# Q loaded on 64 partitions by nine tokens per pair of heads, in an attention and feed-forward kernel

## The chip, the cores and the metric

The kernel runs on one core of a Trainium2 chip. The metric is the device time of one execution in microseconds. TensorE (PE) does the matmuls; VectorE (DVE), ScalarE (ACT) and GpSimd (POOL) work on elements; SyncE (SP) here only issues transfers. Transfers go through 16 DMA engines, in queues that SP, ACT and POOL feed.

## What is computed

```
q, k, v: (8, 8, 576, 64)           # batch, head, token, head_dim; f32
q_s = softmax of q over the 64 elements of a token's head
k_s = softmax of k over the 576 tokens, per element
kv  = einsum('bhsd,bhse->bhde', k_s, v)
x   = einsum('bhsd,bhde->bhse', q_s, kv)   # then (batch * token, head * 64) = (4608, 512)
h   = x @ w_in                     # (512, 2048)
g   = where(h > 0, h, exp(min(h, 0)) - 1)
out = g @ w_out                    # (2048, 512)
```

## The kernel before

One batch is 576 tokens. Its first 512 (`SM`) make one **block** of the feed-forward, and the 64 tokens left over of each of the eight batches (`SR`) are gathered in `XTR` and make a ninth block. A block has 16 steps. In step s, `hidden` makes 128 of the 2048 hidden units for 512 tokens (four matmuls of 128x512 with `W1S`, line 778), ACT takes the exp, POOL a minus one, `elu` on DVE writes `GT`, and `project`, some three steps later, adds that chunk to the four output banks (four matmuls with `W2S`, line 799). After the sixteenth projection `store` copies the four banks to `OSB` and SP writes each of them out, 128 rows of 512 floats.

The attention of batch j+1 is made while block j runs, by **words** in tables: `FIRST` for block 0, `SECOND` for block 1, `LATER` for the others with `CHANGED` over it in block 2. Each step has three strings of words: done after `hidden`, after `project`, and after `elu`. `START` is the list for batch 0, which runs ahead of everything. Every engine works in the order in which the words are met, and `op` puts the waits in by itself, from what was last written and read. So the order of the words is the order of every queue, SP's among them: a transfer on SP's queue that has to wait for a buffer holds those behind it.

The words that matter here:

- `load:Q:2:MR` loads q of batch j+2 (lines 265 to 284). Part A is heads 0 to 3, B is 4 to 7, M both. A partition holds four tokens in a row of each head: 1024 bytes in a piece, 128 partitions. Part R is the 64 tokens left over, in two loads of 64 partitions with 256 bytes a piece. K and V are loaded in the same way. `QR` and `KR` have two buffers, `VR` one.
- `qmax`, `qsub`, `qexp`, `qsum`, `qmul` are the softmax of q, in parts of heads; `qmul` writes `QS` in float16, `qmulr` the rest piece `QSR`.
- `turn:A`, `turn:B`, `turn:R` transpose `QS` to `QW` by DMA on SP's queue, eight, eight and two blocks of 128x128; `wide` copies them to `QT` in float32. `pturn` and `pwide` do the same by TensorE and a bank, for batches 0 and 1.
- `peak`, `join`, `kout`, `kin` find the maximum of k per element and spread it over the partitions through a scratch in DRAM (`kmax_scratch`). For batches 0 and 1 it is done by `kmax`, `kturn`, `kacross`, `diag` and, for batch 1, `kspread`, on DVE and TensorE.
- `ksub`, `kexp`, `vconv`, `kv`, `kfac` make the 64x64 matrices of the heads, in `MB`.
- `att:f` and `xc:f` apply `MB` to a pair of heads' 512 tokens and copy the result to `XT`; `rest0` and `rcopy0` do the rest tokens. `flat:0` to `flat:4` with `xflat` go over the four pairs' 2304 columns in five cuts, rest tokens among them, and `xrest` takes these out to `XTR`. Batches 0 and 1 have the first form, the others the flat one.
- `w1:a:b` and `w2:a:b` load weights on POOL's queue; `warm` runs matmuls on constants; `hold` makes SP wait for the last `hidden`.

Of the kernel before, what the change touches and what calls it, by code (L numbers as in the profile page):

```python
# [27 lines left out]
AB = 7  # L28
# [6 lines left out]
AT = {"rawA": 0, "rawA2": 1, "rawB": 5, "rawB2": 2, "rawS": 6, "rawT": 3,  # L35
      "kturnA": 6, "kturnB": 7, "kvA": 3, "kvB": 6, "pturnA": 7, "pturnB": 3,
      "att0": 5, "att1": 7, "att2": 6, "att3": 4}
START = ("load:K:0:A kmax:A warm:2:6 kraw:A load:Q:0:A load:K:0:R load:K:0:B qmax:A qsub:A:gp kmax:S "
         "kturn:A kacross:A load:V:0:R warm:4:5 qexp:A kmax:B kraw:S load:Q:0:B kmax:T qmax:2 "
         "kturn:B diag:act:A kacross:B load:V:0:B diag:act:B w1:2:4 qmax:3 kraw:T kmin:S w1:0:2 "  # L40
         "kmin:T kmin:A w1:4:6 qsub:2:gp qexp:2 qsum:A kraw:B kexp:T vconv:B:gp kexp:S qsub:3:gp "
         "kmin:B qmul:A:dve kexp:A qexp:3 await:gp:DGA qsum:2 vconv:R:gp load:V:0:A qsum:3 w2:0:1 "
         "kexp:B vconv:A:gp w2:1:2 w1:6:8 pturn:A w2:2:3 kv:A pwide:A:act kfac:A:dve qmul:3:dve "
         "warm:1:5 kv:B att:0 qmul:2:dve att:1 xc:0 load:K:1:R pturn:B kfac:B:dve w2:3:5 load:K:1:M "
         "xc:1 pwide:B:act h:2:4 await:sp:VBA w1:8:10 w2:5:9 att:3 att:2 load:Q:1:A h:0:2 w1:10:14 "
         "xc:2 kmax2:B xc:3 load:Q:0:R kmax2:A kmax2:R ")
FIRST = {
    0: ("", "", ""),
    1: ("qmax:A", "", "load:Q:1:B"),
    2: ("", "", ""),  # L50
    3: ("qsub:0", "qsub:1:dve", ""),
    4: ("", "qexp:A", "qmax0:R qsub0:R:dve"),
    5: ("kturn qsum:A load:Q:1:R kacross w2:9:12", "qexp0:R", "qmul:A"),
    6: ("diag w1:14:16 qmax:C", "qsub:2:dve hold", "qsub:D:dve"),
    7: ("", "", "load:V:1:RAB"),
    8: ("kspread copy", "qexp:C qsum0:R", "ksub:3 qmulr0:dve"),
    9: ("ksub:0 pturn:A", "ksub:2:dve qsum:C", "pwide:A:act"),
    10: ("", "pturn0:R ksub:1:dve ksub:R pwide0:R:act", "vconv:R"),
    11: ("qmul:B:dve rest0", "w2:12:13 vconv:A:dve rcopy0:act", "kexp:A"),
    12: ("pturn:B load:K:2:MR qmulr:gp", "", "kexp:R pwide:B:act hold"),  # L60
    13: ("kv:A load:Q:2:ABR w2:13:16 kfac:A:dve kexp:B", "vconv:B:gp att:0", "xc:0 turn:R peak2:A"),
    14: ("kv:B peak2:R kfac:B:dve", "peak2:B att:1 join2", "xc:1"),
    15: ("att:3 xc:3", "att:2 load:V:2:MR", "kout2 xc:2"),
}
SECOND = {
    0: ("qmax:A", "qsub:1:dve qsub:0", ""),
    1: ("wide0:R:dve qmax:C", "qsub:D", "qexp:A"),
    2: ("rest0", "kin", ""),
    3: ("", "", "qsub:2"),
    4: ("qexp:C", "qsum:A qmul:0", ""),  # L70
    5: ("", "qsum:C", "ksub:R:dve ksub:3"),
    6: ("ksub:2:dve", "load:K:2:MR vconv:B", ""),
    7: ("", "qmulr:dve", "load:Q:2:MR qmul:1"),
    8: ("", "qmul:B:dve", "peak2:A vconv:R"),
    9: ("", "turn:R ksub:A kexp:B", "vconv:A"),
    10: ("kexp:R", "kexp:A", "turn:B"),
    11: ("", "peak2:B", "turn:A wide:R:gp rcopy0:act"),
    12: ("", "wide:B:act wide:A:gp kv:AB", "kfac:AB:dve"),
    13: ("", "flat:0 peak2:R", "xflat:0:act"),
    14: ("flat:1 xflat:1:dve load:K:3:MR", "join2 flat:2", "xflat:2:act"),  # L80
    15: ("flat:3", "xflat:3:dve flat:4", "qmax2:A xflat:4:act load:V:2:MR kout2 xrest:gp"),
}
LATER = {
    0: ("qsub:2", "", ""),
    1: ("qsub:1:dve", "kin", ""),
    2: ("qsub:0", "", ""),
    3: ("", "qexp:A ksub:R:dve ksub:0:dve", "qsum:A"),
    4: ("", "qsub:D", "kexp:R qmul:A:dve"),
    5: ("", "turn:A", "vconv:B"),
    6: ("ksub:3 qexp:C", "ksub:1 vconv:R", "vconv:A"),  # L90
    7: ("ksub:2:dve", "qsum:C", "qmulr:dve qmul:B:dve"),
    8: ("load:V:2:MR kexp:A", "kexp:B", ""),
    9: ("turn:R", "", "wide:A:gp turn:B"),
    10: ("kv:AB kfac:AB:dve", "peak2:A", ""),
    11: ("flat:0 xflat:0:act", "load:Q:3:MR", "peak2:B wide:R:act"),
    12: ("wide:B:dve", "flat:1 peak2:R xflat:1:act", ""),
    13: ("join2 load:K:3:MR", "", "flat:2 qmax2:C xflat:2:act"),
    14: ("", "flat:3 kout2", "xflat:3:act qmax2:A"),
    15: ("flat:4", "xflat:4:act", "xrest:dve"),
}  # L100
CHANGED = {
    0: ("", "", "qmax:C qsub:0"),
    2: ("", "", "qsub:2 load:Q:2:MR"),
# [13 lines left out]
class Gen:  # L117
# [57 lines left out]
    def alloc(self):  # L175
# [89 lines left out]
    def load(self, which, b, parts, en="sp"):  # L265
# [3 lines left out]
        t, e = bufs[s], self.E[en]  # L269
        for part in parts:  # L270
# [299 lines left out]
    def qgroups(self, part):  # L570
        return {"A": slice(0, 16), "B": slice(16, 32), "R": slice(32, 36), "C": slice(16, 36),
                "D": slice(24, 36)}.get(part) or slice(8 * int(part), 8 * int(part) + 8)

    def qstat(self, name, part):
        cells = {"A": "01", "B": "23", "C": "23R", "D": "3R"}.get(part, part)
        return [f"{name}{x}" for x in cells]

    def qkeys(self, b, part):
        s = b % 2
        r = [f"QR{s}R0", f"QR{s}R1"]  # L580
        cells = {"A": "01", "B": "23", "C": "23", "D": "3", "R": ""}.get(part, part)
        return [f"QR{s}{x}" for x in cells] + (r if part in "RCD" else [])

    def qmax(self, b, part):
        v, QR, g = self.E["dve"], self.QR[b % 2], self.qgroups(part)
        self.op("dve", lambda: v.tensor_reduce(self.QM[:, g], QR[:, g, :], AX.X, ALU.max),  # L586
                self.qkeys(b, part), self.qstat("QM", part))

    def qsub(self, b, part, en="gp"):
        e, QR, g = self.E[en], self.QR[b % 2], self.qgroups(part)  # L590
        n = g.stop - g.start
        m = self.QM[:, g].unsqueeze(2).broadcast_to([128, n, 64])
        keys = self.qkeys(b, part)
        self.op(en, lambda: e.tensor_tensor(QR[:, g, :], QR[:, g, :], m, ALU.subtract),  # L594
                keys + self.qstat("QM", part), keys)

    def qexp(self, b, part):
        a, QR, g = self.E["act"], self.QR[b % 2], self.qgroups(part)
        keys = self.qkeys(b, part)
        self.op("act", lambda: a.activation(QR[:, g, :], QR[:, g, :], AF.Exp), keys, keys)  # L600

    def qsum(self, b, part):
        v, QR, g = self.E["dve"], self.QR[b % 2], self.qgroups(part)
        self.op("dve", lambda: v.tensor_reduce(self.QZ[:, g], QR[:, g, :], AX.X, ALU.add),  # L604
                self.qkeys(b, part), self.qstat("QZ", part))
        self.op("dve", lambda: v.reciprocal(self.QI[:, g], self.QZ[:, g]),
                self.qstat("QZ", part), self.qstat("QI", part))

    def qmul(self, b, part, en="gp"):
        e, QR = self.E[en], self.QR[b % 2]  # L610
        g = self.qgroups(part)
        h0, n = g.start // 4, (g.stop - g.start) // 4
        src = QR[:, g, :].rearrange("p (h r) d -> p h r d", r=R)
        z = self.QI[:, g].rearrange("p (h r) -> p h r", r=R).unsqueeze(3).broadcast_to([128, n, R, 64])
        out = self.QS[h0 // 4][:, :, h0 % 4:h0 % 4 + n, :].rearrange("p r h d -> p h r d")
        keys = self.qkeys(b, part)
        cells = {"A": "01", "B": "23"}.get(part, part)
        self.op(en, lambda: e.tensor_tensor(out, src, z, ALU.mult),  # L618
                keys + self.qstat("QI", part), [f"QS{x}" for x in cells])

    def qmul_rest(self, b, en="gp"):
        e, QR = self.E[en], self.QR[b % 2]
        z = self.QI[:, 32:36].unsqueeze(2).broadcast_to([128, 4, 64])
        self.op(en, lambda: e.tensor_tensor(self.QSR[:, :, :], QR[:, 32:36, :], z, ALU.mult),
                self.qkeys(b, "R") + ["QIR"], ["QSR"])

    def qturn(self, part):

        sp = self.E["sp"]
        if part in "AB":  # L630
            hh = 0 if part == "A" else 1
            src = self.QS[hh][:, :, :, :].rearrange("p r h d -> p (r h d)")
# [24 lines left out]
    def qwide_first(self, part, bank, en="act"):  # L657
# [377 lines left out]
```

## Time and profile before

| what | value |
|---|---|
| time, median of 3 runs | 314.96 us (314.33 to 315.04) |
| the profiled execution: time, span | 315.17 us, 313.4 us |
| mean granted TensorE clock | 0.995 |
| first `hidden` matmul of block 0 | 20.1 us |
| first issue of the stores of blocks 0 to 6 | 66.3, 98.5, 129.9, 161.2, 192.5, 223.8, 255.1 us |
| first `hidden` matmul of the ninth block | 278.3 us |
| DMA: moved, mean rate | 51.63 MB, 165 GB/s |
| q loads, by DMA issue: 1024 KB, 512 KB, 64 KB | 5 of 6.7 us, 6 of 5.6 us, 16 of 6.5 us to landing |
| output stores: 256 KB | 2.8 us to landing |

The span is from the first to the last instruction of the profiled execution; the time has a little more around it. The stores of a block are issued in step 3 of the next one, so their distance is the length of a block: 31.3 us from the third on. "To landing" is from the issue of a transfer to its last byte, a median over those of one shape.

### The profile page before, as it was taken

The page shows a single profiled execution, that of the slowest core. Times are in us where ns is not written, and L with a number is a line of the kernel's source. Part 1 is how long each engine was busy: PE and PEld are TensorE (multiplying, and loading weights), DVE is VectorE, ACT ScalarE, POOL GpSimd, SP SyncE. Part 2 cuts the span into 40 slices and gives each one's busy share as a digit, 9 for nine tenths or more (in the row PEclk, how much of TensorE's full clock was granted, in tenths as well). Part 3 has the DMA queues.
Part 4 walks back from the last instruction along what each step waited for, and adds up shares of the span by engine and source line. Part 5 has one row for each costly group of instructions (what it writes and reads, how often), then busy time and mean ns, then how long its engine had stood idle before and what let it go on. Part 6 is the DMA issues. An engine that isn't in the chain of part 4 may idle for free.

```text
span 313.4 us, 4541 instructions
## 1 busy us (share of the span) xinstructions
PE 300.6 (96%) x1604; PEld 238.2 (76%) x1604; DVE 246.6 (79%) x422; ACT 178.8 (57%) x298; POOL 165.8 (53%) x224
## 2 busy tenths in 40 slices
PE   5988789999999999999999999999999999999995
PEld 2557567688878878887888788878888888888884
DVE  6897798989898999899989998999898353435531
ACT  1675558465846855685568556855685543334432
POOL 2975847277725843684368436843684233333330
PEclk9999979999999999999999999999999999999999
DMA  8999996959784897429842974270422030003003
GB/s 234 325 353 337 367 349 189 285 172 284 156 238 149 207 279 216 147 61 238 253 152 56 270 221 153 51 191 1 157 47 42 0 127 9 0 2 135 0 1 134
DMA packets 65079, 51.63 MB, mean 165 GB/s; under 512 B 29344, under 2 KB 57248, under 8 KB 65056
## 3 DMA queue, kind: packets, MB, share of 16 engines
q1 hardware_dynamic: 57984, 41.23, 47.1%
q0 software_dynamic: 5872, 8.39, 9.9%
q10 hardware_dynamic: 1200, 1.72, 1.6%
q8 instruction: 12, 0.20, 0.3%
q14 instruction: 11, 0.09, 0.1%
HBM read 38.27 MB, written 9.45 MB: 152 GB/s over the span
## 4 chain that ended last, share of the span: by engine, by line
PE 85%; DMA 6%; POOL 4%; SPq 2%; DVE 1%; issue 1%; ACT 1%; DVEq 0%
PE bank L799 41%; PE bank L778 39%; DMA QR<-in_q_dram 6%; PE bank L709 2%; PE bank L535 1%; POOL QR L594 1%; SPq L276 1%; POOL VB L515 1%; DVE QM L586 1%; POOL W1S L253 1%; SPq L284 0%; POOL W2S L260 0%; PE bank L687 0%; PE bank L652 0%; PE bank L539 0%
## 5 line engine op out<-in xcount | busy, mean ns | idle before, releaser
L767 POOL TENSOR_SCALAR ES<-ES 128x512 f32<-128x512 f32 x144 | 92.0, 641 | 130.0 <-ACT ES L766 129.8
L799 PE MATMUL bank<-W2S,GT 128*128 128x512 f32 x576 | 156.2, 395 | 1.1 <-DVE GT L789 0.8
L778 PE MATMUL bank<-XT,W1S 128*128 128x512 f32 x512 | 139.6, 394 | 2.7 <-DVE GT L789 2.4
L766 ACT ACTIVATE ES<-bank 128x512 f32<-128x512 f32 x144 | 85.1, 597 | 95.6 <-PE bank L778 95.3
L789 DVE SCALAR_TENSOR_TENSOR GT<-bank,ES 128x512 fp32r<-128x512 f32 x144 | 97.7, 680 | 50.1 <-PE bank L778 39.0
L799 PEld LDWEIGHTS bank<-W2S,GT 128*128 128x128 f32 x576 | 107.2, 189 | 23.6 <-DVE GT L789 1.2
L778 PEld LDWEIGHTS bank<-XT,W1S 128*128 128x128 f32 x512 | 95.0, 189 | 23.4 <-DVE GT L789 2.9
L594 POOL TENSOR_TENSOR QR<-QR,QM 128x512 f32<-128x512 f32 (+2 forms) x22 | 26.5, 1205 | 6.2 <-DVE QM L586 6.2
L600 ACT ACTIVATE QR<-QR 128x1024 f32<-128x1024 f32 (+3 forms) x18 | 19.0, 1057 | 12.1 <-POOL QR L594 7.7
L586 DVE TENSOR_REDUCE QM<-QR 128x16 f32<-128x1024 f32 (+3 forms) x18 | 21.7, 1205 | 2.1 <-DMA QR<-in_q_dram 2.1
L604 DVE TENSOR_REDUCE QZ<-QR 128x16 f32<-128x1024 f32 (+3 forms) x18 | 21.7, 1204 | 0.0
L731 ACT ACTIVATE XT<-bank 128x512 fp32r<-128x512 f32 (+2 forms) x28 | 15.4, 551 | 10.9 <-PE bank L709 10.9
L414 POOL TENSOR_TENSOR KR<-KR,NB 128x512 f32<-128x512 f32 (+1 forms) x14 | 21.3, 1539 | 0.0
L618 DVE TENSOR_TENSOR QS<-QR,QI 128x1024 f16<-128x1024 f32 (+1 forms) x15 | 18.5, 1241 | 0.0
L778 PE MATMUL bank<-XTR,W1S 128*128 128x512 f32 x64 | 16.6, 389 | 0.0
L367 DVE TRANSPOSE_TENSOR_REDUCE KM<-KR 128x32 f32<-128x1024 f32 x12 | 14.8, 1234 | 0.0
L452 ACT ACTIVATE EK<-KR 128x1024 bf16<-128x1024 f32 x14 | 14.2, 1056 | 0.4 <-POOL KR L414 0.4
L778 PEld LDWEIGHTS bank<-XTR,W1S 128*128 128x128 f32 x64 | 12.0, 188 | 2.5
L517 ACT ACTIVATE VB<-VR 128x1024 bf16<-128x1024 f32 x12 | 12.7, 1056 | 0.1
L709 PEld LDWEIGHTS bank<-QT,MB 128*128 128x128 f32 x48 | 8.9, 188 | 4.0 <-DVE MB L566 0.5
L709 PE MATMUL bank<-QT,MB 128*128 128x320 f32 (+5 forms) x48 | 11.5, 300 | 0.0
L414 DVE TENSOR_TENSOR KR<-KR,NB 128x512 f32<-128x512 f32 x13 | 11.0, 847 | 0.2
(96 smaller groups left out, 202.8 us busy)
## 6 DMA issues: line engine op xcount, KB each, us to landing
out_dram<-OSB SPq DMA_DIRECT2D x35, 256.0 KB, 2.8
KR<-in_k_dram SPq DMA_DIRECT2D x7, 1024.0 KB, 8.1
VR<-in_v_dram SPq DMA_DIRECT2D x6, 1024.0 KB, 5.8
QR<-in_q_dram SPq DMA_DIRECT2D x5, 1024.0 KB, 6.7
QR<-in_q_dram SPq DMA_DIRECT2D x6, 512.0 KB, 5.6
W1S<-in_moe_w_in_dram POOLq DMA_DIRECT2D x6, 512.0 KB, 10.3
VR<-in_v_dram SPq DMA_DIRECT2D x4, 512.0 KB, 8.8
W2S<-in_moe_w_out_dram POOLq DMA_DIRECT2D x2, 768.0 KB, 9.1
```

Of the source, the lines that this page charges most:

```text
L414: self.op(en, lambda: e.tensor_tensor(kv, kv, m, ALU.subtract), keys + ["NB"], keys)
L586: self.op("dve", lambda: v.tensor_reduce(self.QM[:, g], QR[:, g, :], AX.X, ALU.max), self.qkeys(b, part), self.qstat("QM", part))
L594: self.op(en, lambda: e.tensor_tensor(QR[:, g, :], QR[:, g, :], m, ALU.subtract), keys + self.qstat("QM", part), keys)
L600: self.op("act", lambda: a.activation(QR[:, g, :], QR[:, g, :], AF.Exp), keys, keys)
L604: self.op("dve", lambda: v.tensor_reduce(self.QZ[:, g], QR[:, g, :], AX.X, ALU.add), self.qkeys(b, part), self.qstat("QZ", part))
L618: self.op(en, lambda: e.tensor_tensor(out, src, z, ALU.mult), keys + self.qstat("QI", part), [f"QS{x}" for x in cells])
L709: last = pe.matmul(self.bank[bank][:, a - c0:b - c0], self.MB[f][:, :, :].rearrange("p u d -> p (u d)"), self.QT[:, f, a - f * S:b - f * S ...
L766: self.op("act", lambda: a.activation(ES[:, :], ps, AF.Exp), [f"bank{bank}"], [ek])
L767: self.op("gp", lambda: g.tensor_scalar(ES[:, :], ES[:, :], -1.0, 1.0, ALU.add, ALU.mult), [ek], [ek])
L778: return pe.matmul(ps, self.W1S[:, kc, c * 128:(c + 1) * 128], x[:, kc, 0:SM], start=(kc == 0), stop=(kc == 3))
L789: self.op("dve", lambda: v.scalar_tensor_tensor(self.GT[n % NG][:, :], ps, 0.0, ES[:, :], ALU.max, ALU.min), [f"bank{bank}", ek], [f"GT{n ...
L799: return pe.matmul(self.bank[OB[t]][:, :], self.GT[n % NG][:, t * 128:(t + 1) * 128], self.W2S[:, c, :], start=(c == 0), stop=(c == NCH - 1))
```

## The change

- Q is loaded in four pieces, 0 to 3, each of them two heads (0 and 2, 1 and 3, 4 and 6, 5 and 7). Head a of the piece has partitions 64a to 64a+63, and a partition holds nine tokens in a row: 2304 bytes. There is no part R; a batch has four loads for three.
- The tokens of a block are so another set: those with place 0 to 7 of every nine (`QF` = 8), and the ninth is the rest token. The output rows follow: a store writes two places of 64 partitions, as 2 x 64 rows.
- The softmax of q runs over parts of 18 columns (A, B) or nine (one piece), rest tokens among them; only batch 0 keeps a part R of its own.
- `turn` has nine blocks for A and for B, and no R. `wide` copies 1152 columns each.
- Batch 1 takes the flat attends and the scratch for its maximum of k. In `START` the warming matmuls are gone.
- All tables have new words: other steps for the same work, other parts between the engines, and other places of the loads.

```diff
+QP = 64
+QN = S // QP
+QF = SM // QP
...
-START = ("load:K:0:A kmax:A warm:2:6 kraw:A load:Q:0:A load:K:0:R load:K:0:B qmax:A qsub:A:gp kmax:S "
...
+START = ("load:K:0:A load:Q:0:0 load:K:0:R kmax:A kmax:S load:Q:0:1 qmax:A load:K:0:B kraw:S "
+         "load:V:0:A qsub:A:gp kturn:A load:Q:0:2 kacross:A kmax:B qmax:2 kmax:T w1:2:4 diag:act:A "
+         "qexp:A qsum:A load:Q:0:3 qsub:2:gp vconv:A:act qmax:3 load:V:0:R qsub:3:gp kraw:T kraw:A "
+         "kmin:A kturn:B kmin:S w1:0:2 vconv:R:gp qexp:2 kacross:B load:V:0:B kexp:A kraw:B "
+         "load:K:1:M load:Q:1:1 qsum:2 w2:0:1 qmul:A:dve w1:4:6 qmul:2:gp kexp:S diag:act:B kmin:B "
+         "kv:A qexp:3 kexp:B kmin:T pturn:A kexp:T vconv:B:dve await:sp:VBB qsum:3 pwide:A:act "
+         "kfac:A:dve load:Q:1:0 qmul:3:dve kv:B kfac:B:dve w2:1:3 att:0 w1:6:8 xc:0 w2:3:4 att:1 "
+         "pturn:B pwide:B:act xc:1:dve h:2:4 w1:8:11 w2:4:6 att:2 w2:6:9 xc:2 att:3 w1:11:14 h:0:2 "
+         "xc:3 await:sp:bank5 load:K:1:R ")
 FIRST = {
...
+    0: ("peak:A qmax:A peak:B", "peak:R", ""),
+    1: ("load:Q:1:3 w1:14:16", "join", ""),
+    2: ("load:Q:1:2 qsub:0 kout qsub:1:dve", "", ""),
...
+    6: ("qsum0:R hold kin load:V:1:RAB", "qsub:2", ""),
+    7: ("pturn:A", "qmul0:R:dve", "ksub:R:dve pwide:A:act"),
...
 LATER = {
...
-    8: ("load:V:2:MR kexp:A", "kexp:B", ""),
-    9: ("turn:R", "", "wide:A:gp turn:B"),
-    10: ("kv:AB kfac:AB:dve", "peak2:A", ""),
-    11: ("flat:0 xflat:0:act", "load:Q:3:MR", "peak2:B wide:R:act"),
...
+    6: ("kexp:R", "ksub:3:dve turn:A ksub:2", "vconv:A"),
+    7: ("vconv:R kexp:A", "qsum:B peak2:R", "kexp:B load:Q:3:1"),
+    8: ("", "", ""),
+    9: ("", "peak2:A kv:AB qmul:B", "turn:B kfac:AB:dve"),
+    10: ("wide:A:act", "load:Q:3:3", ""),
+    11: ("join2", "load:V:2:MR flat:0", "wide:B:dve xflat:0:act load:Q:3:2"),
+    12: ("qmax2:A flat:1", "", "xflat:1:act"),
+    13: ("flat:2", "kout2 load:K:3:MR", "xflat:2:act"),
+    14: ("", "", "load:Q:3:0 flat:3 xflat:3:act"),
+    15: ("qmax2:B flat:4", "xflat:4:act", "xrest:dve"),
 }
 CHANGED = {
-    0: ("", "", "qmax:C qsub:0"),
-    2: ("", "", "qsub:2 load:Q:2:MR"),
+    0: ("", "", "qmax:B qsub:0"),
+    2: ("", "", "qsub:2 load:Q:2:0 load:Q:2:1 load:Q:2:2 load:Q:2:3"),
 }
...
+        if which == "Q":
+            for x in "".join({"A": "01", "B": "23", "M": "0123"}.get(x, x) for x in parts):
+                dst = t[:, QN * int(x):QN * (int(x) + 1), :].rearrange("p r d -> p (r d)")
+                frm = src[b, 4 * (int(x) // 2) + int(x) % 2::2, :, :][0:2].rearrange("a (p r) d -> a p (r d)", r=QN)
+                cells = [f"QR{s}{x}", f"QR{s}R{x}"]
+                self.op(en, lambda: e.dma_start(dst, frm), (), cells, dma=f"d_{cells[0]}")
+            return
...
-            src = self.QS[hh][:, :, :, :].rearrange("p r h d -> p (r h d)")
-            dst = self.QW[hh][:, :, :, :].rearrange("p r j t -> p (r j) t")
...
+        sp, hh = self.E["sp"], "AB".index(part)
+        src = self.QS[hh][:, :, :, :].rearrange("p r u d -> p (r u d)")
+        self.op("sp", lambda: sp.dma_start_transpose(self.QW[hh][:, :, :], src),
+                [f"QS{x}" for x in "0123"[2 * hh:2 * hh + 2]], [f"QW{part}"], dma=f"d_QW{part}")
...
         for t in range(4):
-            rows = self.out[j * S:j * S + SM, :].rearrange("(p r) c -> r p c", r=R)[t]
+            rows = self.out[j * S:(j + 1) * S, :].rearrange("(p r) c -> r p c", r=QN)[2 * t:2 * t + 2]
             self.op("sp", lambda: sp.dma_start(rows, self.OSB[t][:, :]),
                     [f"OSB{t}{x}" for x in ("", 0, DM // 2)], [], dma=f"d_OSB{t}")
...
-        rows = self.out.rearrange("(b s) c -> s b c", s=S)[SM:S, 2 * t:2 * t + 2, c0:c1]
+        rows = self.out.rearrange("(b p r) c -> r p b c", p=QP, r=QN)[QF, :, 2 * t:2 * t + 2, c0:c1]
```

More of the change, by code (lines that the diff above doesn't have):

```diff
@@ L64 @@
 }
 SECOND = {
[L66 to L81, printed above, removed]
+    0: ("qmax:A load:Q:2:0 load:K:2:MR qmax:B qsub:0", "qsub:1:dve", ""),
+    1: ("", "qexp:A", "qsub:3:dve"),
+    2: ("qsub:2", "", "kin"),
+    3: ("qsum:A", "vconv:R", ""),
+    4: ("", "vconv:A qmul:1:dve", "vconv:B ksub:R:dve"),
@@ new lines @@
+    5: ("ksub:2:dve", "", ""),
+    6: ("qmul:0 peak2:B", "qexp:B", "ksub:3:dve"),
+    7: ("", "peak2:A", "ksub:A"),
+    8: ("kexp:B kexp:R", "turn:A peak2:R qsum:B", ""),
+    9: ("kexp:A", "", "load:Q:2:1 load:Q:2:2"),
+    10: ("load:K:3:MR", "kv:AB wide:A:act qmul:B", ""),
+    11: ("kfac:AB:dve join2", "", "qmax2:A"),
+    12: ("", "flat:0", "xflat:0:act"),
+    13: ("turn:B", "", "flat:1 wide:B:act"),
+    14: ("xflat:1:dve load:Q:2:3 load:V:2:MR", "flat:2", "xflat:2:act kout2"),
+    15: ("flat:3 xflat:3:dve", "flat:4 xflat:4:act", "xrest:gp"),
@@ L96 @@
[L96 to L99, printed above, removed]
+    0: ("qsub:0", "", ""),
+    1: ("kin", "vconv:B:gp", "qsub:1"),
+    2: ("", "qsub:2", ""),
+    3: ("peak2:B", "", "qexp:A ksub:1"),
+    4: ("", "qsum:A ksub:R:dve qsub:3", ""),
+    5: ("qexp:B", "", "qmul:A ksub:0:dve"),
+    6: ("kexp:R", "ksub:3:dve turn:A ksub:2", "vconv:A"),
@@ L568, in kv_fac, with qcells @@
                 ALU.mult, ALU.mult), [f"bank{bank}", f"KZ{f // 2}", "MASK"], [f"MB{f}"])
[L570 to L582, printed above, removed]
+    def qcells(self, b, part):
+        slots = {"A": "01", "B": "23", "R": "0123"}.get(part, part)
+        if part == "R":
+            return [f"R{x}" for x in slots]
+        return list(slots) + ([f"R{x}" for x in slots] if b else [])
@@ L584, in qmax, with qkeys, qview @@
+    def qkeys(self, name, b, part):
+        return [f"{name}{x}" for x in self.qcells(b, part)]
+    def qview(self, t, b, part):
+        v = t.rearrange("p (s r) d -> p s r d", r=QN) if len(t.shape) == 3 else \
+            t.rearrange("p (s r) -> p s r", r=QN)
+        if part == "R":
+            return v[:, :, QF:QN]
+        s0, n = {"A": (0, 2), "B": (2, 2)}.get(part) or (int(part), 1)
+        return v[:, s0:s0 + n, 0:QN if b else QF]
     def qmax(self, b, part):
-        v, QR, g = self.E["dve"], self.QR[b % 2], self.qgroups(part)
@@ L591, in qsub @@
[L591 to L595, printed above, removed]
+        e, QR = self.E[en], self.qview(self.QR[b % 2][:, :, :], b, part)
+        m = self.qview(self.QM[:, :], b, part).unsqueeze(3).broadcast_to(list(QR.shape))
+        keys = self.qkeys(f"QR{b % 2}", b, part)
+        self.op(en, lambda: e.tensor_tensor(QR, QR, m, ALU.subtract),
+                keys + self.qkeys("QM", b, part), keys)
@@ L604, in qsum @@
[L604 to L607, printed above, removed]
-    def qmul(self, b, part, en="gp"):
[L610 to L619, printed above, removed]
@@ L641, in qturn_first @@
-    def qturn_first(self, part, bank):
+        v, QR = self.E["dve"], self.qview(self.QR[b % 2][:, :, :], b, part)
+        z, i = (self.qview(t[:, :], b, part) for t in (self.QZ, self.QI))
+        self.op("dve", lambda: v.tensor_reduce(z, QR, AX.X, ALU.add),
+                self.qkeys(f"QR{b % 2}", b, part), self.qkeys("QZ", b, part))
+        self.op("dve", lambda: v.reciprocal(i, z),
+                self.qkeys("QZ", b, part), self.qkeys("QI", b, part))
+    def qmul(self, b, part, en="gp"):
+        e, QR = self.E[en], self.qview(self.QR[b % 2][:, :, :], b, part)
+        z = self.qview(self.QI[:, :], b, part).unsqueeze(3).broadcast_to(list(QR.shape))
+        reads = self.qkeys(f"QR{b % 2}", b, part) + self.qkeys("QI", b, part)
+        if part == "R":
+            out, keys = self.QSR[:, :, :].unsqueeze(2), ["QSR"]
+        else:
+            s0, n = {"A": (0, 2), "B": (2, 2)}.get(part) or (int(part), 1)
+            out = self.QS[s0 // 2][:, 0:QN if b else QF, s0 % 2:s0 % 2 + n, :].rearrange("p r u d -> p u r d")
+            keys = [f"QS{s0 + x}" for x in range(n)]
+        self.op(en, lambda: e.tensor_tensor(out, QR, z, ALU.mult), reads, keys)
@@ L646, in qturn_first @@
-        n = src.shape[1]
-        def mm():
-            for j in range(2):
-                for r in range(n):
-                    o = (j * n + r) * 128
-                    last = pe.transpose(ps[:, o:o + 128], src[:, r, 2 * j:2 * j + 2, :]
-                                        .rearrange("p u d -> p (u d)"), self.ID16[:, :])
+        if part == "R":
+            src = [self.QSR[:, 2 * x:2 * x + 2, :] if b == 0 else self.QS[x][:, QF, :, :] for x in range(2)]
+            reads = ["QSR"] if b == 0 else [f"QS{x}" for x in range(4)]
+        else:
+            hh = "AB".index(part)
+            src = [self.QS[hh][:, r, :, :] for r in range(QF)]
+            reads = [f"QS{2 * hh + x}" for x in range(2)]
@@ L654, in mm @@
+        def mm():
+            for i, x in enumerate(src):
+                last = pe.transpose(ps[:, i * 128:(i + 1) * 128], x.rearrange("p u d -> p (u d)"),
+                                    self.ID16[:, :])
             return last
-        self.op("pe", mm, (["QSR"] if part == "R" else [f"QS{x}" for x in {"A": "01", "B": "23"}[part]]) + ["ID16"], [f"bank{bank}"])
+        self.op("pe", mm, reads + ["ID16"], [f"bank{bank}"])
     def qwide_first(self, part, bank, en="act"):
-        a = self.E["act"]
@@ new lines, in qwide_first @@
+            src = ps[:, 0:4 * QP].rearrange("p (f t) -> p f t", f=4)
+        else:
+            hh = "AB".index(part)
+            out = self.QT[:, 2 * hh:2 * hh + 2, 0:SM].rearrange("p a (r t) -> p a r t", t=QP)
+            keys = [f"QT{part}"]
+            src = ps.rearrange("p (r a t) -> p a r t", a=2, t=QP)
+        self.copy(en, out, src, [f"bank{bank}"], keys)
+    def qwide(self, part, en="act"):
+        hh = "AB".index(part)
+        out = self.QT[:, 2 * hh:2 * hh + 2, :].rearrange("p a (r t) -> p a r t", t=QP)
+        src = self.QW[hh][:, :, :].rearrange("p r (a t) -> p a r t", a=2)
+        self.copy(en, out, src, [f"QW{part}"], [f"QT{part}", f"QTR{part}"])
@@ L713, in attend_flat @@
         fs = [x // 2 for x in VISIT[v]]
[L714 to L715 removed]
+        halves = sorted({"AB"[f // 2] for f in fs})
+        self.op("pe", mm, [f"MB{f}" for f in fs] + [f"QT{x}" for x in halves] +
+                ([f"QTR{x}" for x in halves] if v else []), [f"bank{bank}"])
     def xcopy_flat(self, b, v, bank, en="act"):
@@ L743, in mm @@
             return last
-        self.op("pe", mm, [f"MB{f}" for f in range(4)] + ["QTR"], [f"bank{bank}"])
+        self.op("pe", mm, [f"MB{f}" for f in range(4)] + ["QTRA", "QTRB"], [f"bank{bank}"])
     def xcopy_rest(self, b, bank, en="act"):
```

119 lines of the change are left out of this document (30 added, 89 removed).

## The prediction

> **What bounds the kernel now.** First the span and the busy shares, then the chain of work that ended last, on the page of the kernel before:
>
> ```profile
> span 313.4 us, 4541 instructions
> PE 300.6 (96%) x1604; PEld 238.2 (76%) x1604; DVE 246.6 (79%) x422; ACT 178.8 (57%) x298; POOL 165.8 (53%) x224
> ...
> DMA  8999996959784897429842974270422030003003
> ...
> PE 85%; DMA 6%; POOL 4%; SPq 2%; DVE 1%; issue 1%; ACT 1%; DVEq 0%
> ```
>
> TensorE is the bound: 96% busy, 85% of the chain. The DMA row is full for the first six slices (47 us), while weights and three batches arrive, and about half full later. So there is a second resource with a start where it binds and, later, room. How much room one steady block has is read from the DMA view of 161.2 to 192.5 us, from one block's stores to the next block's:
>
> ```profile
> q1 hardware_dynamic: 7728, 5.18, 59.4%
> q10 hardware_dynamic: 176, 0.26, 2.5%
> ...
> out_dram<-OSB SPq DMA_DIRECT2D x4, 256.0 KB, 3.7
> ```
>
> Columns: packets, MB, share of 16 engines. With 0.6% of two small queues this is 62.5% of 31.3 us, 19.6 us of work for each of the 16 engines in a block of 31.3 us. The reader is to see that this is a mean: it hides every transfer as long as the work lies evenly on the 16.
>
> How it is spread before: on the page, ACT's own queue carries
>
> ```profile
> q10 hardware_dynamic: 1200, 1.72, 1.6%
> ```
>
> It has six NB loads of 128 rows, six scratch stores of 16 rows and one last half store of 128 rows: 992 rows. 1200 - 992 = 208 = 13 x 16. Each of the 13 transfers has 16 packets more than its rows, even the one with 16 rows of 128 bytes. So each was ended on 16 engines, and a transfer was cut by its outermost rows, not by bytes.
>
> **The change, part by part.** *Outermost counts.* Before, both sides of every transfer begin with the same count: 128, 64 or 16. After, the DRAM side of each q load counts 2 heads x 64 partitions x 576 elements against 128 partitions in SBUF, and the DRAM side of each store of `store` counts 2 x 64 x 512 against 128. If transfers are cut by the outermost row, only two pieces fit both sides, of 64 packets each. That has no row in the trace: the bounds are 16 engines (8 packets each, the row of 3.7 us to landing above) and two. I take two, because the 16-row transfer shows the cut by rows. Nor does a row tell which two; I take the same two each time, the costlier end. [...]
>
> *Price of a packet.* The DMA view of 255.8 to 258.8 us holds stores alone:
>
> ```profile
> GB/s 0 191 328 382 355 328 355 410 410 437 383 355 328 355 410 382 437 410 382 301 328 382 382 437 410 382 382 300 328 328 383 355 437 382 355 382 382 328 219 82
> DMA packets 570, 1.04 MB, mean 348 GB/s; under 512 B 61, under 2 KB 61, under 8 KB 570
> ...
> q1 hardware_dynamic: 570, 1.04, 95.4%
> ```
>
> 95.4% of 16 x 3.0 us is 45.8 us for 509 packets of 2 KB: 0.090 us each. The best slice, 437 GB/s, is 27.3 per engine: 0.075 us. With 14 engines mostly idle beside them I take 0.080, nearer the best. A q packet of 2304 bytes is never seen; by bytes it is 0.090 (0.084 at the best slice's rate; at 17.7 KB per us, the mean of the loads of 0.5 to 9 us, mostly 1 KB and 256 B packets, 0.130 at the worst). So a q load is 64 x 0.090 = 5.8 us and a store 64 x 0.080 = 5.1 us on each of the two engines.
>
> *Per block on these two:* q 4 x 5.8 = 23.0; stores 4 x 5.1 = 20.5; the rest stays spread. That is 19.6 less the stores' 512 x 0.090 / 16 = 2.9 and q's 1.18 MB at this block's 17.4 KB per us (5.18 MB in 59.4%), 4.2: 12.5. Together 56 us, where the block of TensorE takes 31.3. The two engines become the bound.
>
> *Where it ends.* All of SP's transfers share its queue in order, so k, v and the transposes wait on these two as well. The order in the program: in block j (from the second on) the four stores of block j-1, then transpose A of the next batch, q pieces, transpose B, and v, k and q pieces between; block 2 issues eight q loads. I take the two engines as never idle until the last piece of q(7), as their backlog starts with q(0) and q(1). Work up to there: q 32 x 5.8 = 184; stores of blocks 0 to 3, 16 x 5.1 = 82; the rest 7.5 x 12.5 = 94; weights 9.9% of 313.4 (the page's software queue) = 31; with 2 us before the first packet, 393. Behind transpose B of block 4 stand three q pieces, k and v (17.3 + 8.3), so it lands at 367. Then one copy (1.0) and three steps of 1.81 (a pair of 0.91 in the chain): block 4 ends at 374. Its stores wait for the queue, 393 to 413. Transpose (1.5), copy (1.0) and steps 11 to 15 with their attends (10): block 5 ends at 426. Block 6: 7 us to the stores, 20.5, 12.5: 466. Block 7 has no next batch: 29.7, as before (248.6 to 278.3); then 35.1 to the end, as before: 531. Outside the span the profiled run had 315.17 - 313.4 = 1.8: 533 us. That run is 0.2 above the median 314.96, nothing beside this.
>
> *TensorE's own part.* In block 0 four turns of K (0.6 us), the spread of NM (0.4) fall away, two small transposes come (0.1), and the flat attends stream the same 2304 columns as four attends and the rest pieces. 0.9 us less. Seven warming matmuls lay in waits for loads: 0. All this is hidden under the queue: 0 in the sum; it is worth 0.9 only where TensorE binds.
>
> *Rest pieces.* Seven small transposes (1.2 us of SP each), their multiplications and copies fall away, the two remaining ones have nine blocks for eight; reductions and exps are in two of 18 columns for 16 and 20. DVE, ACT and POOL were 79, 57 and 53% busy, so 0. Batch 1's maximum of K goes through the scratch (3.3 and 3.0 us to landing) in place of kspread, issued in steps 2 and 6 of block 0 and used from step 7; hidden while q(1) is later still. The waits of SP for VBB and bank 5 in START hold only k(1) and q(1) pieces back, with q(0) still on the two engines: 0.
>
> *Bounds.* Best: 0.075 and 0.084, and the rest at five sixths: q 172, stores 77, rest 78, weights 26 give 355, and the same walk 492. Worst in reason: 0.090, and 0.110 for q (between 0.101 by bytes and 0.130): q 225, stores 92, which with 94, 31 and 2 gives 444 and 589 at the end. Gaps in the queue at hand-overs add; an engine alone that beats the best slice takes off.
>
> **Rivals.** *A: all 16 engines still carry each transfer* (or another pair each time). For it: every row of before ends on 16. Against: none of them has an outer count below 16. Then q is lighter (512 packets for 1536 a batch), and what remains is TensorE: -0.9 us, and of the first block's stalls, 2.6 us idle from 30 to 40 us and 3.4 us at half clock (0.83 in 40 to 50 us), up to 4.3 us, as the late q pieces (14.0 us in the chain) come in one piece; the pieces of q and v now ahead of the first attends can cost 1 to 2. Middle: 311, faster. It decides where the two busiest engines have under 31 us a block.
>
> *B: the cut follows one side only.* If loads alone go to two engines, the stores cost 2.9 a block: 184 + 12 + 94 + 31 + 2 = 323, transpose B at 297, block 4 ends at 304, blocks 5 and 6 at 31.3 each, then 64.8: 433. If stores alone do, each of blocks 1 to 6 waits at flat:0, nominally 22 us in, for 7 + 20.5 + 2.5 = 30: 6 x 8 = 48, 363. For it: source or destination might rule; against: both ends have to be cut.
>
> **How the numbers follow.** Forecast 0.87, B 0.07 (both slower), A 0.06. Predicted: 533. A run here can tell 0.3% from no change. Slower by more than that: 0.87 + 0.07 = 0.94; A I split 0.05 faster, 0.01 same. The range is that of the unknown prices with room for gaps, 470 to 600: about 0.92 of the forecast's cases, 0.80 of all. The cases outside it are far off and not reached.
>
> **What would show it.** Right: the DMA row has a mean of two engines' worth (an eighth) plus the spread work, never full, while SP's loads and stores take 5 to 7 us on an idle queue and tens behind others; the chain names DMA and SP ahead of PE; PE idles in blocks 0 to 6 at the flat attends, waiting for QT; blocks 7 and 8 keep 29.7 and 35.1 us; the granted clock falls below 0.995. Stores land in 5 us or more even in block 8. Wrong: stores land in about 3 us and the blocks stay at 31.3 us (A); or only one of the two kinds is slow (B). If loads and stores are as priced but the blocks are shorter than 50 us, they don't share the two engines.

## The result and the profile after

The changed kernel takes 519.12 us (median of four runs, 518.34 to 520.13); the kernel before took 315.00 us beside it (314.33 to 315.42). The ratio is 1.649, 95% interval 1.645 to 1.653. The forecast was 533 us with a range of 470 to 600. Where the runs of one kernel lie more than 1.5% apart (`b_outer8` below: 331.5 and 333.9 us, and 336.6 twice), the time and the ratio given are those of the faster ones.

From the page of the changed kernel: the span, the busy shares, two rows of the picture in 40 slices (each 13.0 us), the two hardware queues and the chain.

```profile
span 518.3 us, 4516 instructions
PE 328.4 (63%) x1594; PEld 255.8 (49%) x1594; DVE 239.8 (46%) x403; ACT 177.3 (34%) x287; POOL 190.5 (37%) x236
...
PEclk9975685896996699555998589957997899699999
DMA  4459926445274911189519762296319218101012
...
q1 hardware_dynamic: 48496, 41.16, 40.8%
q10 hardware_dynamic: 1376, 1.98, 1.4%
...
DMA 32%; PE 26%; SPq 24%; DVE 6%; POOL 6%; ACT 4%; issue 2%; DVEq 0%
```

No engine is busier than 63%. The chain, which was 85% TensorE, is now 56% DMA and SP's queue. TensorE's own work grew from 300.6 to 328.4 us though it has ten matmuls fewer: the granted clock is 5 to 8 tenths in many slices, 0.832 on average.

What TensorE stood still for is in the waits of the changed kernel (waiting group, releaser: us in total, times, longest):

```profile
ACT QT L728 <- DMA QW<-QS: 122.1, 7, 37.2
PE bank L705 <- ACT QT L728: 111.9, 7, 36.4
```

L705 are the flat attends: seven waits, one in each of seven blocks, 16 us on average, for the copy QT, which waits for the transpose on SP's queue. What that queue does shows in the timeline of SP over two blocks (start, us to issue, line, operation):

```profile
259.16 16.01 SPq L814 DMA_DIRECT2D out_dram<-OSB  x4
275.21 9.09 SPq L639 DMA_TRANSPOSE QW<-QS  x1
...
313.71 16.80 SPq L814 DMA_DIRECT2D out_dram<-OSB  x4
330.55 10.29 SPq L639 DMA_TRANSPOSE QW<-QS  x1
```

In these two blocks the four stores stand in front of the transpose and take 16 us to be issued at all, then the transpose 9 to 10; from one block's stores to the next's it is 54.6 us, where TensorE needs 31.3.

That a store is on two engines is seen where nothing else moves, from 459 to 485 us, the stores of block 6 (DMA view: GB/s in 40 slices; then packets, MB, share of 16 engines):

```profile
GB/s 0 0 0 44 32 25 25 44 50 50 50 50 50 50 57 50 50 50 50 50 50 50 50 57 50 50 50 50 50 50 50 57 50 50 50 50 38 0 0 0
DMA packets 521, 1.06 MB, mean 41 GB/s; under 512 B 8, under 2 KB 8, under 8 KB 520
...
q1 hardware_dynamic: 520, 1.05, 11.0%
...
out_dram<-OSB SPq DMA_DIRECT2D x4, 256.0 KB
```

512 rows of 2 KB and 8 packets under 512 B: each of the four transfers ends with two small packets, not 16. The rate is 50 GB/s, 25 for each of two engines, against 348 on average in the stores-only window of the kernel before. The packets run from 461.2 to 482.9 us: 21.7 us, 5.4 a store. 11.0% of 16 x 26 us is 45.8 us of packet time, 2.1 packets at any moment of these.

### The profile page after: what moved, and what is told of

It is laid out like the page before. It is cut to its first block, busy times and chain, and to the rows that moved or that the text cites. A ratio compares the mean times of both kernels' runs of the same rounds, so it can differ in the third digit from the quotient of the medians.

```text
span 518.3 us, 4516 instructions
## 1 busy us (share of the span) xinstructions
PE 328.4 (63%) x1594; PEld 255.8 (49%) x1594; DVE 239.8 (46%) x403; ACT 177.3 (34%) x287; POOL 190.5 (37%) x236
## 3 DMA queue, kind: packets, MB, share of 16 engines
q1 hardware_dynamic: 48496, 41.16, 40.8%
## 4 chain that ended last, share of the span: by engine, by line
DMA 32%; PE 26%; SPq 24%; DVE 6%; POOL 6%; ACT 4%; issue 2%; DVEq 0%
PE bank L775 12%; PE bank L796 11%; DMA QW<-QS 11%; DMA KR<-in_k_dram 9%; SPq L277 8%; SPq L639 7%; DMA QR<-in_q_dram 7%; SPq L285 5%; DMA VR<-in_v_dram 3%; SPq L293 3%; POOL ES L764 2%; DMA W2S<-in_moe_w_out_dram 2%; POOL QR L607 2%; DVE GT L786 2%; DVE KR L434 1%
## 5 line engine op out<-in xcount | busy, mean ns | idle before, releaser
L775 PE MATMUL bank<-XT,W1S 128*128 128x512 f32 x512 | 153.7, 426 | 31.1 <-DVE GT L786 30.9
L796 PE MATMUL bank<-W2S,GT 128*128 128x512 f32 x576 | 163.2, 409 | 13.4 <-DVE GT L786 13.0
L775 PEld LDWEIGHTS bank<-XT,W1S 128*128 128x128 f32 x512 | 103.4, 208 | 57.9 <-DVE GT L786 35.5
L705 PE MATMUL bank<-QT,MB 128*128 128x320 f32 (+5 forms) x56 | 17.5, 379 | 113.4 <-ACT QT L728 111.9
L705 PEld LDWEIGHTS bank<-QT,MB 128*128 128x128 f32 x56 | 13.3, 243 | 120.6 <-issue 114.6
L607 POOL TENSOR_TENSOR QR<-QR,QM 128x576 f32<-128x576 f32 (+3 forms) x29 | 33.7, 1162 | 56.8 <-DVE QM L600 56.8
L728 ACT ACTIVATE QT<-QW 128x1152 fp32r<-128x1152 f16 x7 | 8.1, 1162 | 122.1 <-DMA QW<-QS 122.1
L600 DVE TENSOR_REDUCE QM<-QR 128x18 f32<-128x1152 f32 (+3 forms) x18 | 21.9, 1215 | 58.4 <-DMA QR<-in_q_dram 58.4
L633 POOL TENSOR_TENSOR QS<-QR,QI 128x1152 f16<-128x1152 f32 (+2 forms) x15 | 30.7, 2047 | 1.1 <-DVE QI L620 1.1
L613 ACT ACTIVATE QR<-QR 128x1152 f32<-128x1152 f32 (+3 forms) x18 | 19.0, 1057 | 16.9 <-DVE QR L607 10.4
L618 DVE TENSOR_REDUCE QZ<-QR 128x18 f32<-128x1152 f32 (+3 forms) x18 | 21.7, 1208 | 0.8 <-ACT QR L613 0.7
L728 ACT ACTIVATE XT<-bank 128x512 fp32r<-128x512 f32 (+2 forms) x33 | 18.2, 550 | 10.6 <-PE bank L705 10.6
## 6 DMA issues: line engine op xcount, KB each, us to landing
W1S<-in_moe_w_in_dram POOLq DMA_DIRECT2D x5, 512.0 KB, 17.1
```

The source lines that it names most:

```text
L607: self.op(en, lambda: e.tensor_tensor(QR, QR, m, ALU.subtract), keys + self.qkeys("QM", b, part), keys)
L633: self.op(en, lambda: e.tensor_tensor(out, QR, z, ALU.mult), reads, keys)
L705: last = pe.matmul(self.bank[bank][:, a - c0:b - c0], self.MB[f][:, :, :].rearrange("p u d -> p (u d)"), self.QT[:, f, a - f * S:b - f * S ...
L728: self.op("act", lambda: e.activation(out, src, AF.Copy), reads, writes)
L775: return pe.matmul(ps, self.W1S[:, kc, c * 128:(c + 1) * 128], x[:, kc, 0:SM], start=(kc == 0), stop=(kc == 3))
L796: return pe.matmul(self.bank[OB[t]][:, :], self.GT[n % NG][:, t * 128:(t + 1) * 128], self.W2S[:, c, :], start=(c == 0), stop=(c == NCH - 1))
```

## The experiments

**Cutting the q loads and the stores back to 64 outer rows.** In all three kernels the layout, the order of the work and the flat attends are those of the change. Only the transfers differ: `e_both16` issues each q load as two of 64 partitions (one a head), and each store as two of 64 rows, `e_loads16` does the first alone, `e_stores16` the second alone. The diff is shortened.

```diff
-  frm = src[b, 4*(x//2) + x%2 :: 2, :, :][0:2].rearrange("a (p r) d -> a p (r d)", r=QN)
-  e.dma_start(t[:, QN*x:QN*(x+1), :], frm)
+  for i in range(2):
+      frm = src[b, 4*(x//2) + x%2 + 2*i, :, :].rearrange("(p r) d -> p (r d)", r=QN)
+      e.dma_start(t[64*i:64*i+64, QN*x:QN*(x+1), :], frm)
...
-  sp.dma_start(rows[2*t:2*t+2], OSB[t][:, :])
+  for i in range(2):
+      sp.dma_start(rows[2*t + i], OSB[t][64*i:64*i+64, :])
```

> The changed kernel, with each q piece as two loads of 64 partitions (one head each) and each store as two of 64 rows: same bytes, same packets, same words, but every outermost count is 64. Theory (two of 16 engines carry these transfers because the outermost count is 2): blocks of 31 us again, near 311 us, 16 end packets a transfer. Rival (the new words and the order of the loads make the stalls): over 450 us, since neither is touched. Rival (2304-byte packets or scattered rows are slow in themselves): over 450 us.

> Only the loads of q cut into two of 64 partitions; the stores keep the outermost count 2. Theory: the stores alone burden two engines with 21 us a block beside 12.5 of spread work, the attends wait some 8 us in each of blocks 1 to 6: 363 us. Rival (the loads were all of it): 311. Rival (the loads' shape has no part): about 519.

> Only the stores cut into two of 64 rows; the loads of q keep the outermost count 2. Theory: 184 us of q on two engines beside 137 of spread work, blocks 0 to 4 bound by them, the later ones by TensorE: 433 us. Rival (the stores were all of it): 311. If loads and stores went to different pairs of engines, the parts over 311 of this run and of the one with the loads cut would not add up to the 208 of the whole, but the larger would be the whole.

Measured: both cut 326.62 us (ratio 1.036, 1.032 to 1.041), loads cut alone 393.38 (1.242 to 1.257), stores cut alone 435.87 (1.376 to 1.393). The page of `e_both16`, the same rows:

```profile
span 326.2 us, 4583 instructions
PE 300.0 (92%) x1594; PEld 236.5 (73%) x1594; DVE 239.2 (73%) x403; ACT 177.6 (54%) x287; POOL 194.0 (59%) x236
...
q1 hardware_dynamic: 50416, 41.17, 51.3%
...
PE 75%; DMA 8%; DVE 7%; POOL 5%; ACT 1%; SPq 1%; issue 1%; ACTq 0%; DVEq 0%
```

The bytes and rows are the same, and 192.5 of the 204 us are gone. q1 has 50416 - 48496 = 1920 packets more. 32 loads and 32 stores were cut, so it is 30 each: two transfers of 16 end packets where one with 2 was. It is the outer count, then, that set the time, and the number of engines with it.

With one kind left on two engines the time is 66.8 us (stores) and 109.3 us (loads) above 326.6, together 176, near the 192.5 of both. The chain of `e_loads16`, by engine and by line, and its waits:

```profile
PE 44%; DMA 29%; POOL 13%; DVE 4%; SPq 4%; ACT 3%; issue 1%; ACTq 0%; DVEq 0%
DMA QW<-QS 23%; PE bank L784 21%; PE bank L805 20%; POOL ES L773 5%; POOL QR L616 4%; SPq L280 3%; PE bank L714 2%; DMA KR<-in_k_dram 2%; POOL QS L642 2%; DMA W2S<-in_moe_w_out_dram 2%; ACT QT L737 2%; DMA QR<-in_q_dram 2%; POOL KR L432 1%; POOL VB L533 1%; ACT ES L772 1%
```

```profile
ACT QT L737 <- DMA QW<-QS: 62.3, 7, 11.8
PE bank L714 <- ACT QT L737: 53.0, 7, 11.1
```

and the chain of `e_stores16`:

```profile
PE 35%; DMA 33%; SPq 14%; POOL 9%; DVE 4%; ACT 3%; issue 2%; DVEq 0%; ACTq 0%
PE bank L775 17%; PE bank L796 16%; DMA QR<-in_q_dram 14%; DMA KR<-in_k_dram 7%; DMA VR<-in_v_dram 7%; SPq L277 6%; SPq L285 5%; DMA QW<-QS 5%; POOL ES L764 3%; POOL QS L633 2%; SPq L293 2%; POOL QR L607 2%; DVE GT L786 1%; POOL KR L423 1%; SPq L639 1%
```

With narrow stores the transpose behind them is late (23% of the chain). With narrow loads q itself, and K and V that are queued with it, are late (14, 7 and 7%).

That the two costs add up could also mean that SP's queue runs one transfer after the other, on whichever engines. The packet records speak against it: q's packets have 2304 bytes and those of a store 2048, so they can be told apart. In the changed kernel, with both kinds narrow, they are under way together for 0.5 us in the whole run. The stores of block 4 are issued from 368.5 us on, while the last q piece runs from 371.6 to 377.6, and their first packet starts at 377.4. With one kind spread over 16 the two do run side by side on the same queue, for 5.8 us in `e_loads16` and 17.1 in `e_stores16`. Narrow loads and narrow stores wait for the same engines.

**The outer count put into the kernel before.** Layout, order and rest pieces are those of before. Only the main q loads (one a head) and the stores are dealt so that their outermost count is OUTER; rows stay as long as they were. The diff is shortened.

```diff
+  e.dma_start(t[:, 4*h:4*h+4, :], src[b, h, 0:SM, :].rearrange("(p a r) d -> a p (r d)", a=OUTER, r=R))
...
-  rows = out[j*S:j*S+SM, :].rearrange("(p r) c -> r p c", r=R)[t]
+  rows = out[j*S:j*S+SM, :].rearrange("(p a r) c -> r a p c", a=OUTER, r=R)[t]
```

Loads and stores deal the tokens to the partitions in the same new way.

> The kernel before with its own words and 1024-byte runs, but tokens dealt so that partition 64a+p has tokens 4(2p+a) to 4(2p+a)+3 of a batch: q's main loads (one a head) and the stores then have an outermost count of 2, and nothing else changes. Theory: on the two engines 512 packets of 0.046 us for q and 256 of 0.084 for stores a block beside 12.5 us, 57 us: 480 to 540 us. Rival (the new words, or pieces of 2304 bytes): the time before, 315 to 320.

> The kernel before, with its main q loads and its main stores dealt so that the outermost count of the DRAM side is 4 instead of 2. If the outermost count says how many engines share a transfer: on the four engines a block has 11.8 us of q, 10.8 us of stores and 12.5 us of its own share of the rest, 35 us against the block's 31.3, so 325 to 365 us, and 8 end packets a store. Rival, the pattern itself (two strided dimensions) is what is slow: about 520 us as with a count of 2.

> The same with an outermost count of 8. By the count of engines: 5.9 + 5.4 + 12.5 = 24 us a block on the eight, under the block's 31.3, so hidden: 315 to 320 us. By the rival (the pattern): about 520 us.

> The same with an outermost count of 16, the control: same number of transfers and of rows in the same pattern, on all engines. By the count of engines 315 to 318 us; by the rival about 520 us.

Measured: 523.14 us for 2 (1.652 to 1.671 of before), 377.82 for 4 (1.196 to 1.203), 332.7 for 8 (the mean of 331.5 and 333.9; 1.052 to 1.060), 319.65 for 16 (1.013 to 1.017). The count of 2 came out as expected; 4 and 8 took 13 us more than the upper ends given (365 and 320), and 16 took 2 more than 318, far from the rival's 520. The page of `b_outer2`:

```profile
span 521.3 us, 4604 instructions
PE 326.5 (63%) x1604; PEld 254.7 (49%) x1604; DVE 246.3 (47%) x422; ACT 180.3 (35%) x298; POOL 170.9 (33%) x224
...
PE 44%; SPq 28%; DMA 19%; DVE 4%; POOL 3%; issue 1%; ACT 0%; DVEq 0%; POOLq 0%
```

Without any other part of the change, the kernel before is as slow as the changed one. The same pattern at 16 costs 4.5 us (1.5%), so the pattern isn't slow in itself. The packet records of the traces say it directly. The table, worked out from the start and the length of every packet, has, from 100 us to the end of the last packet, the us during which nothing was under way, and during which exactly as many packets were as the outer count says (16 at most):

```
kernel       outer  nothing  exactly the outer count
before         128    110.9    20.3 (16)
b_outer16       16     98.6    17.4 (16)
b_outer8         8     81.0    37.0 (8)
b_outer4         4     61.2    85.0 (4)
b_outer2         2     42.6   212.0 (2)
changed          2     39.7   185.9 (2)
e_both16        64     99.8    24.2 (16)
```

In the changed kernel exactly 4 are under way for 6.6 us only. The number of packets in flight follows the count.

The sizes of the steps in between were not all right. The timeline of SP in `b_outer4`, the stores of blocks 0 to 4:

```profile
88.30 3.31 SPq L830 DMA_DIRECT2D out_dram<-OSB  x4
133.79 3.14 SPq L830 DMA_DIRECT2D out_dram<-OSB  x4
179.28 4.85 SPq L830 DMA_DIRECT2D out_dram<-OSB  x4
214.38 4.80 SPq L830 DMA_DIRECT2D out_dram<-OSB  x4
248.80 3.35 SPq L830 DMA_DIRECT2D out_dram<-OSB  x4
```

Blocks 3 and 4 take 35.1 and 34.4 us, where 35 was worked out. But the first stores come at 88.3 instead of 66.3 us, and blocks 1 and 2 take 45.5 each: 22 + 13 + 14 us that the expectation did not have. In the profiled run of `b_outer8`, 336.6 us and so 4 above the time given, the excess of 21 us lies there alone (first stores 14.1 us later, blocks 1 and 2 4.3 and 2.9 longer, then 31.3 as before). In that of `b_outer16` the first stores come 4.7 us later, and 3.7 of these are there at the first `hidden` matmul (23.8 us for 20.1): in START SP takes 2.60 and 2.54 us to issue parts A and B of q, one transfer a head, where one transfer each took 0.49 and 0.60. So what the smaller count adds to the first block is 9.5 us for 8 and 17 us for 4 (first stores at 80.5 and 88.3, for 71.0 with 16). The expectation priced the steady block and not the start, where the DMA row of the kernel before is at 8 and 9.

**The 12 us that cut transfers leave.** `e_both16` should have taken 311 us and took 326.6. Its stores come at 73.0 us for 66.3 before, and its blocks take 32.4 for 31.3. Its waits have one line that grew most, DVE's GT for POOL's ES; before and then `e_both16`:

```profile
DVE GT L789 <- POOL ES L767: 4.6, 8, 1.2
```

```profile
DVE GT L795 <- POOL ES L773: 18.7, 22, 1.7
```

Of the 6.7 us at the first stores 1.8 are there at the first `hidden` matmul already (21.9 us for 20.1). Two causes were tried: the multiplication of q by its scale (QS), which the change runs on POOL in most blocks, and loads that come late in block 0 (the R loads of k(1), W2 chunks).

```diff
@@ e_qmul (some of its six places)
-    4: ("qsum:A qsub0:R", "qmul:A", "qexp0:R"),
+    4: ("qsum:A qsub0:R", "qmul:A:dve", "qexp0:R"),
...
-    5: ("qexp:B", "", "qmul:A ksub:0:dve"),
+    5: ("qexp:B", "", "qmul:A:dve ksub:0:dve"),
...
-    9: ("", "peak2:A kv:AB qmul:B", "turn:B kfac:AB:dve"),
+    9: ("", "peak2:A kv:AB qmul:B:dve", "turn:B kfac:AB:dve"),
@@ e_start
-         "load:K:1:M load:Q:1:1 qsum:2 w2:0:1 qmul:A:dve w1:4:6 qmul:2:gp kexp:S diag:act:B kmin:B "
+         "load:K:1:M load:K:1:R load:Q:1:1 qsum:2 w2:0:1 qmul:A:dve w1:4:6 qmul:2:gp kexp:S diag:act:B kmin:B "
...
-         "xc:3 await:sp:bank5 load:K:1:R ")
+         "xc:3 await:sp:bank5 ")
...
-    2: ("load:Q:1:2 qsub:0 kout qsub:1:dve", "", ""),
+    2: ("load:Q:1:2 qsub:0 w2:9:11 kout qsub:1:dve", "", ""),
...
-    8: ("w2:9:11 load:K:2:MR ksub:1:dve", "qexp:B pturn0:R pwide0:R:act w2:11:13", ""),
+    8: ("load:K:2:MR ksub:1:dve", "qexp:B pturn0:R pwide0:R:act w2:11:13", ""),
```

`e_tuned` has both.

> The changed kernel with q loads and stores cut to an outermost count of 64 (which took 326.6 us), and with two more edits: the multiplications of q by the scale of A, B and block 0 moved from POOL to DVE, and the R loads of k(1) and the last three W2 chunks issued earlier. Theory: POOL's 2.07 us multiplications delay ES and so GT and TensorE by 1.1 us in each of some six blocks, and the two late loads cost 6.7 us in block 0: 312 to 316 us. Rival: the 12 us come from the order of the flat attends itself: stays at 325 to 327.

Measured: 341.78 us (1.083 to 1.089 of before): both the theory and its rival missed, and it is slower by 15. So the two edits were run apart:

> The changed kernel with q loads and stores cut to an outermost count of 64 (326.6 us), and of the two further edits only the earlier issue: k(1)'s R loads right behind its M loads, the last three W2 chunks in step 2 instead of 8. With both edits 341.8 us. Theory now: the multiplications on DVE cost what was lost, and the late loads cost up to 6.7 us in block 0, so 320 to 325 us and block 0's stores issued at 66 to 71 instead of 73.0. Rival: block 0 is late for another reason, and the time stays at 326 to 328.

> The same base (326.6 us), and of the two edits only the multiplications of q by the scale moved from POOL to DVE. Theory: DVE's queue is the tighter one, each 1.3 us multiplication ahead of a GT holds TensorE: blocks of 35 us instead of 32.4, 340 to 345 us. Rival: the 341.8 us came from the earlier issue of the loads, and this one takes 320 to 327.

Measured: `e_start` 328.39 us (1.037 to 1.047), no gain, near its rival's 326 to 328; `e_qmul` 343.71 (1.087 to 1.099), as its theory said. The 15 us are those of the multiplications. One steady block in windows (us; busy us of PE, PEld, DVE, ACT, POOL with instructions; granted clock, DMA share, GB/s), before:

```profile
129.94:161.22 31.28, 31.28 (x177) 25.66 (x177) 29.43 (x51) 20.32 (x34) 17.43 (x23) 1.00 0.67 175
```

`e_both16`:

```profile
136.99:169.41 32.42, 31.86 (x177) 25.61 (x177) 27.50 (x47) 20.03 (x33) 23.06 (x26) 1.00 0.70 171
```

`e_qmul`:

```profile
140.54:175.84 35.30, 32.37 (x177) 25.45 (x177) 30.38 (x49) 20.12 (x33) 20.39 (x24) 1.00 0.63 155
```

With the multiplications DVE has 30.4 us of work in a block, only 1 more than before, but the block is 4 us longer, and TensorE is idle for 2.9 us of it; in `e_tuned`, whose blocks take the same 35.3, TensorE's waits for GT at L784 are 12.6 us in the whole run, for 2.8 in `e_both16` (weight loads 18.2 for 4.9). So DVE's total doesn't price the move; that it is what DVE does just ahead of a GT fits these waits, but no run moves one multiplication alone. The theory of `e_tuned` fell: POOL, at 2.2 us a multiplication in these blocks, is a cheaper place in this order than DVE at 1.3.

`e_start` took one wait away and did not come out ahead. Its first stores are at 72.9 us instead of 73.0. TensorE's timeline in `e_start` (start, us, what, with the idle time before it and its releaser):

```profile
31.42 2.00 PE L805 MATMUL bank<-W2S,GT 128*128 128x512 f32 x4 [3.72 <-DVE GT L795]
...
49.41 1.20 PE L784 MATMUL bank<-XT,W1S 128*128 128x512 f32 x4 [1.32 <-DVE GT L795]
...
53.26 0.61 PE L665 MATMUL bank<-ID,QS 128*128 128x128 f16 x8 [0.53 <-POOL QS L642]
...
56.72 0.28 PE L665 MATMUL bank<-ID,QS 128*128 128x128 f16 x2 [0.54 <-DVE QT L739]
```

The first of these waits was 5.30 us in `e_both16`, so 1.6 us were won, and the wait of 1.9 us for W2 at 54.9 is gone. Waits for q's own chain through POOL and DVE stand in its place, 0.5 us each. Which work is to blame for the 6.7 us of block 0 and the 1.1 us a block stays open: no kernel here removes them, and none that ran is faster than the kernel before. One candidate was not tried: two transfers for one also keep SP longer, 5.0 us for a block's stores where four took 1.8 before, and in `b_outer16`, with the words of before, more transfers in START came with a late first block too.

## Why the prediction was right, and where its sizes were off

- *Two of 16 engines, the same two for all.* Shown: two end packets a transfer, 25 GB/s each, two packets under way for 185.9 us, and 192.5 us regained by nothing but cutting the transfers. If loads and stores had each had a pair of their own, the costlier kind alone, 109.3 us, would have been nearly the whole; instead the two costs add up (66.8 + 109.3 of 192.5), and the packets of the two kinds run side by side for 0.5 us only. Every row of before had 16 engines, so no run then showed a transfer on two: the two was the author's estimate, from how the 208 end packets were read. What the runs showed of it since: with 2, 4, 8 and 16 outer rows exactly 2, 4, 8 and 16 packets are under way for 212.0, 85.0, 37.0 and 17.4 us from 100 us on, where the kernel before has 2.4, 1.1, 2.3 and 20.3. Which two engines they are the records don't name.
- *Prices.* A store was put at 5.1 us and took 5.4 (median packet 0.084 us for 0.080). A q packet has a median of 0.093 for 0.090: 6.0 us a load for 5.8.
- *The walk.* It carried the two engines without a gap to the last q piece. Up to there fewer than two packets were under way for only 4.5 us. Its end, put at 393, is at 377.6 us, 15 us early; the end of the span is 13 us early (531 put, 518.3 measured). The walk adds up packet times as if an engine had one packet under way at a time. By the medians above q and the stores take 32 x 5.95 + 16 x 5.4 = 277 us, 11 more than was put, which leaves 377.6 - 277 - 2 = 99 for the rest (K, V, transposes, weights), where 94 + 31 = 125 was put. But the rest did not shrink: the lengths of its packets up to 377.6 us add up to 181 us per engine, as a mean over 16, and those of q and the stores to 213 and 88 on each of two. That is 481 us in 377.6. So packets of one engine overlap; more than 16 are under way for 117 of these us. The step that was off is the adding: the packet times were put too low and their overlap at nothing. The two work against each other, and that the sum came within 14 us owes something to luck. How much of the two engines' time each kind held the records don't say. Step by step:

| first issue, us | predicted | measured |
|---|---|---|
| stores of block 4 (its end + 7) | 381 | 368.5 |
| stores of block 5 | 433 | 417.0 |
| stores of block 6 | 473 | 460.0 |
| from there to the end | 57.8 | 58.3 |

  From block 6's stores on it is 58.3 us, to a tenth what it was before (255.09 to 313.4): no transpose is left behind the stores.
- *What would show it.* The chain, the waits for QT, the clock and blocks 7 and 8 are as written. The four stores issued in block 8 have their packets from 490.2 to 512.3 us, 5.5 us each; the 2.4 us to landing that the page gives for stores is a median of the ninth block's own alone, whose DRAM side begins with 64 places. "Never full" was wrong: the DMA row has 9 in several slices. The weights still have 16 end packets a transfer (240 for the 15 loads on POOL's queue), and from 38.9 to 51.8 us they nearly alone fill the row, at 299 GB/s; in between stands a 1, at 50 to 52 GB/s up to block 6's stores, the two engines alone, or a 2.
- *Rival B.* Loads alone were put at 433 and took 435.9. Stores alone were put at 363 and took 393.4: a block of 39.3 us was worked out, and blocks of 42 to 45 came. Part of it is that `e_both16` itself needs 32.4 rather than 31.3, and starts 6.7 us late.
- *Rival A.* 311 us was mis-sized; the layout with all 16 engines takes 326.6. Its sum had nothing for the new order of the work ("DVE, ACT and POOL were 79, 57 and 53% busy, so 0") nor for more transfers; with 16 engines blocks take 32.4 us and the first stores come 6.7 us late. Which of the two it is, is not shown. It is not a term of the result itself, where TensorE waits far longer for QT.

## What to carry to other kernels

Read the outermost count of the DRAM side of every transfer, as source and as destination, not only its bytes and its runs: 64-row halves issued apart took 326.6 us where one two-row pattern over the same rows took 519. A mean of 62% busy DMA engines says nothing of room if a few of them carry one stream; look for packets under way, and for the end packets of a transfer. The busy share of an engine doesn't price a move of work to it: look at what then stands in front of the instruction that TensorE waits for. A steady block's sum says nothing of the start, where the transfers of the kernel before are packed most tightly (8 and 9 tenths in the first six slices of its DMA row).

## What the runs showed of the hardware

A narrow transfer is slow without being visible in the total: in the changed kernel all queues together are 50% busy (40.8 + 7.6 + 1.4 and less), yet up to 377.6 us fewer than two packets are under way for only 4.5 us. Behind them SP itself is held: four stores take 9.7 to 16.8 us to issue in blocks 0 to 5, where they took 1.8 to 1.9 in the kernel before. On the same queue wide transfers run beside a narrow one (5.8 and 17.1 us in `e_loads16` and `e_stores16`), but a store and a q load that both have an outermost count of 2 do not run beside each other (0.5 us in all). And a count of 8, half the engines, costs nothing in a steady block of 31.3 us, while in its profiled run the first stores come 9.5 us later than with 16.
